# Segment loop of a recurrent-memory attention kernel: one PSUM tile of six banks, projection units interleaved by row chunk, output columns split 256 + 384

## The chip, the cores and the metric

The kernel runs on one core of a Trainium2 chip. The metric is the device time of one execution in microseconds (us), as a median of runs. The profile is one execution recorded by the hardware profiler; its times are us unless marked ns. Engines are TensorE (PE, with its weight loads as PEld), VectorE (DVE), ScalarE (ACT), GpSimd (POOL) and SyncE (SP).

## The reference, cut to what matters

Two attentions over 2048 rows of width 640 are mixed by a gate. Part B is a sliding, dilated attention. Part A, which the change touches, is a recurrence: 64 segments of 32 rows, each preceded by 8 memory rows that the segment before computed, 32 heads of width 192.

```python
for s in range(n_seg):
    h = jnp.concatenate([mem, x[:, 32*s:32*s + 32]], axis=1)      # 8 + 32 rows
    q, k, v = (jnp.einsum('btd,dhe->bhte', h, W) for W in (Wq, Wk, Wv))
    scores = jnp.einsum('bhqe,bhke->bhqk', q, k) * scale          # masked
    o = jnp.einsum('bhqk,bhke->bhqe', softmax(scores), v)
    o = jnp.einsum('bhte,hed->btd', o, Wo)
    mem = o[:, :8];  outs.append(o[:, 8:])
out = g * concatenate(outs) + (1 - g) * B
```

So segment s + 1 can't start before the memory rows of segment s are there: the 64 segments run one after the other.

## The kernel before, in words

Part B and a prepass (projections of the last 8 rows of each segment, called z, which need no memory) come first; then `part_a` runs the 64 segments in a loop that Python unrolls, and `part_z` finishes the output rows of z. In the loop the order of PE, ACT and DVE is the order in which the code is written; DMAs and POOL are placed by the framework, which also writes the semaphore waits, from which tile each instruction reads and writes.

**Projections.** Q, K and V of a segment are nine units (`q`, `k`, `v`, each with u = 0, 1, 2). A unit is 5 row chunks (kc) of 4 matmuls (L771), which work side by side on four strips of 32 columns and put 128 x 512 sums in one PSUM bank. The weights lie in SBUF, except for 14 pieces of 384 KB (`STREAM`) that are read again in each segment through a ring of five buffers (`get_unit`, L569, on SP's queue).

**Order of one segment.** Units Q0 and K0 begin (L957, L958); `sel_b` (L951) turns the last memory rows into lhsT; Q0, K0, Q1, K1 are finished one after the other, and each is copied out of PSUM by ACT (`c_qk`, L784). Q2 begins, then PE transposes the first four copies (`t_qk`, L792) and DVE places them (`c_t`, L803, L807). K2 follows, then scores of half 0 (`s_a`, `s_b`, L825, L834), exp on ACT (`e_exp`, L843), the DMA of V of z (`load_vz`, L756), the last two transposes, V0, sums (`e_norm`, L857), reciprocal as Ln and Exp on ACT (L862, L863) and two DVE multiplies (L869, L870), the same for half 1, V1, V2, and for each half `pv_half` (L897, L902) with its copies `c_x` (L911) and `c_z` (L918). V's copies (`c_v`, L881) are DVE's. The output product (`o_group`, L940) takes 48 chunks for columns 0 to 383 ("oa") and again for 384 to 639 ("ob"). ACT copies each sum to `whi` (L1030, L1038); from it `sel` makes the next segment's memory rows: chunks 0 to 2 from oa, chunks 3 and 4 from ob. `tail` and `store` finish the output rows.

**PSUM.** Three pools with two buffers each: `psm` (one bank: Q, K, V sums, output sums), `psx` (one bank: transposes, half of `pv_half`, `ps_a`), `psS` (two banks: K0, scores, other half of `pv_half`, `ps_mem`). Each use takes a tile of its own.

Of the kernel before, what the change touches and what calls it, by code (L numbers as in the profile page):

```python
# [14 lines left out]
STREAM = (("k", 0, 2), ("q", 1, 1), ("k", 1, 2), ("q", 2, 1), ("q", 2, 4), ("k", 2, 4), ("v", 0, 0), ("v", 1, 0), ("v", 1, 3),  # L15
          ("v", 2, 2), ("oa", 0), ("ob", 0), ("oa", 5), ("ob", 7))
# [13 lines left out]
class _K:  # L30
# [466 lines left out]
    def weights_setup(self):  # L497
        nc, tc, KC = self.nc, self.tc, self.KC
        rest = []
        for m in "qkv":  # L500
            ks = sorted(range(KC), key=lambda kc: (len(self.units(m, 0, kc)) < 3, kc)) if m == "k" else range(KC)
            rest += [(m, J, kc) for kc in ks for J in range(4)]
        rest += [k for k in [("oa", i) for i in range(12)] + [("ob", i) for i in range(8)] if k not in STREAM]
        n = (0, N_EARLY, -N_MID - N_V - N_LAST, -N_V - N_LAST, -N_LAST, None)
        self.early, *self.late = [rest[n[x]:n[x + 1]] for x in range(5)]
        self.W = {m: W.rearrange("(c p) f -> p c f", p=128) for m, W in zip("qkv", (self.Wq, self.Wk, self.Wv))}
        self.wres = self.ctx.enter_context(tc.tile_pool(name="wres", bufs=1))
        self.res_tiles = {}
        self.ahead = {}
        self.after = mybir.DependencyInfo(mybir.DependencyClass.Sync, mybir.DependencyReason.DATA)  # L510
        self.wstream = self.ctx.enter_context(tc.tile_pool(name="wstream", bufs=WBUFS))
        self.wscr = dict(zip(STREAM, self.dram.tile([len(STREAM), 128, 1536], BF, name="wscr")))

    def tile_of(self, pool, k):
        n = 1536 if k[0] in ("oa", "ob") else 512 * len(self.units(*k))
        t = pool.tile([128, n], BF, name="w_" + "_".join(map(str, k)))
        self.res_tiles[k] = t if n < 1536 or k[0] in ("q", "k", "v") else t[:].rearrange(
            "p (c f) -> p c f", c=4 if k[0] == "oa" else 6)
        return t
# [13 lines left out]
    def wo_slice(self, k, dst):  # L533

        n, f0, f1 = (4, 0, 384) if k[0] == "oa" else (6, 384, 640)
        src = self.Wo.rearrange("(c p) f -> p c f", p=128)[:, :, f0:f1]
        return dst.rearrange("p (c f) -> p c f", c=n), src[:, n * k[1]:n * k[1] + n]

    def wo_place(self, part, c):

        n = 4 if part == "oa" else 6
        return c // n, c % n
# [177 lines left out]
    def part_a(self):  # L720
# [4 lines left out]
        with ctx:  # L725
# [3 lines left out]
            VU = [self.TZ[:, 512 * u:512 * u + 512] for u in range(3)]  # L729
            stage = VU + [self.TZ[:, 1920:2432]]  # L730
            KTz = self.TZ[:, 1536:1920].rearrange("p (c k) -> p c k", k=32)
            E0, Vz, zst = self.TZ[:, 1920:2144], self.TZ[:, 2176:2560], self.TZ[:, 1984:2368]
# [5 lines left out]
            k_runs = ([(0, 4, stage[3])], [(0, 1, self.TZ[:, 2432:2560]), (1, 4, ZB[:, 0:384])], [(0, 4, VU[2])])  # L738
            q_runs = ([(0, 4, 2, 0)], [(0, 2, 2, 16), (2, 4, 1, 0)], [(0, 4, 1, 8)])
            KTs = [[z[:, f0 + 128 * x:f0 + 128 * x + 128] for x in range(n)] for z, f0, n in (  # L740
                (self.TZ, 1920, 5), (ZB, 0, 3), (self.TZ, 1024, 4))]
# [4 lines left out]
            psm = ctx.enter_context(tc.tile_pool(name="psm", bufs=2, space=bass.MemoryType.PSUM, reuse_waits="tile"))  # L746
            psx = ctx.enter_context(tc.tile_pool(name="psx", bufs=2, space=bass.MemoryType.PSUM, reuse_waits="tile"))
            psS = ctx.enter_context(tc.tile_pool(name="psS", bufs=2, space=bass.MemoryType.PSUM, reuse_waits="tile"))
# [14 lines left out]
            for s in range(nseg):  # L763
                pqs, sts, pTs, pSs = {}, {}, {}, {}

                def project(ps, m, u, kcs):
                    for kc in kcs:
                        st = self.get_unit((m, u, kc)) if (m, u, kc) in STREAM else None
                        for j in range(4):
                            rhs = self.res(m, j, kc, 512 * u, 512) if st is None or j == 3 else st[:, 512 * j:512 * j + 512]  # L770
                            nc.tensor.matmul(ps[32 * j:32 * j + 32, :], lhsT=hT[:, kc, :], rhs=rhs, start=(kc == 0),  # L771
                                             stop=(kc == KC - 1), tile_position=(0, 32 * j), skip_group_check=True)

                def m_qk(i, kcs):
                    if i not in pqs:
                        pqs[i] = psS.tile([128, 2, 512], F32, tag="S", name="ps_qk")[:, 0, :] if i == 1 else \
                            psm.tile([128, 512], F32, tag="m", name="ps_qk")
                    project(pqs[i], ("q", "k")[i % 2], i // 2, kcs)

                def c_qk(i):  # L780

                    assert i - 4 not in sts
                    sts[i] = stage[i % 4]
                    nc.scalar.copy(sts[i], pqs[i][:])  # L784
# [34 lines left out]
                def s_a(R, chunks):  # L819
                    h, r = R // 2, R % 2  # L820
                    if h not in pSs:
                        pSs[h] = psS.tile([128, 2, 512], F32, tag="S", name="ps_S")
# [49 lines left out]
                pvs = {}  # L872

                def m_v(u, kcs=range(KC)):
                    if u not in pvs:
                        pvs[u] = psm.tile([128, 512], F32, tag="m", name="ps_v")
                    project(pvs[u], "v", u, kcs)

                def c_v(u):
                    for f0, f1 in ((0, 256), (256, 512)) if u == 1 else ((0, 512),):  # L880
                        nc.vector.tensor_copy(VU[u][:, f0:f1], pvs[u][:, f0:f1])  # L881

                def pv_half(h):
                    E = Es[h]
                    pS = psS.tile([128, 2, 512], F32, tag="S", name="ps_oT")
                    px = [psx.tile([128, 512], F32, tag="x", name="ps_oT") for _ in range(2)]
                    pos = [pS[:, 0], px[0], pS[:, 1], px[1]]
                    po = [pos[j][:, 0:240].rearrange("p (r t q) -> p r t q", r=2, t=3) for j in range(4)]
                    full, half = ((0, 0, 0, 128), (2, 1, 256, 384)), ((1, 0, 128, 192), (1, 1, 192, 256))
                    for r, chunks in ((0, full), (1, full), (2, full), (0, half), (1, half), (2, half)):  # L890
                        for t, par, f0, f1 in chunks:
                            p0 = 64 if f0 == 192 else 0
                            for j in range(4):
                                ks = slice(32 * j, 32 * j + 32)
                                out = po[j][p0:p0 + f1 - f0]
                                if r < 2:
                                    nc.tensor.matmul(out[:, r, t, :], lhsT=V[2 * h + r][ks, f0:f1],  # L897
# [25 lines left out]
                pso = {}  # L923

                def o_group(part, i2):
                    n = 384 if part == "oa" else 256
                    if i2 == 0:
                        pso[part] = psm.tile([128, 512], F32, tag="m", name="ps_wo")
                    for jj in range(4):
# [3 lines left out]
                        if (part, i) not in osl:  # L933
# [5 lines left out]
                            osl[part, i] = w[:].rearrange("p (c f) -> p c f", c=4 if part == "oa" else 6)  # L939
# [6 lines left out]
                def sel(part, hT_next, pm):  # L946

                    m0, m1 = (0, 3) if part == "oa" else (3, KC)
                    p = 0 if part == "oa" else 1
                    for m in range(m0, m1):  # L950
                        nc.tensor.matmul(pm[:, p, 8 * (m - m0):8 * (m - m0) + 8], lhsT=whi[:, m * 128:(m + 1) * 128],  # L951
                                         rhs=self.sel_m[:], start=(m == m0), stop=(m == m1 - 1),
                                         skip_group_check=True)
                    nc.vector.tensor_copy(hT_next[:, m0:m1, 0:8], pm[:, p, 0:8 * (m1 - m0)].rearrange(  # L954
                        "p (m i) -> p m i", i=8))

                m_qk(0, (0, 1, 2))  # L957
                m_qk(1, (0, 1))  # L958
                if sel_b is not None:
                    sel_b()  # L960
                m_qk(1, (2,))
                if tail is not None:
                    tail()
                m_qk(0, (3, 4)); c_qk(0)
                m_qk(1, (3, 4)); c_qk(1)
                if store is not None:
                    store()
                m_qk(2, range(KC)); c_qk(2)
                m_qk(3, range(KC)); c_qk(3)
                m_qk(4, (0, 1))  # L970
# [5 lines left out]
                m_qk(4, (2, 3, 4)); c_qk(4)  # L976
# [3 lines left out]
                m_qk(5, range(KC)); c_qk(5)  # L980
# [3 lines left out]
                load_vz(s)  # L984
# [4 lines left out]
                m_v(0)  # L989
                c_v(0)  # L990
# [10 lines left out]
                m_v(1, (0,))  # L1001
# [4 lines left out]
                m_v(1, (1, 2, 3, 4)); c_v(1)  # L1006
                e_mask(1)
                m_v(2, (0, 1, 2))
                pos = pv_half(0)
                c_x(0, pos, (0, 1, 3), "add")  # L1010
                e_norm(1)
                e_recip_a(1)
                m_v(2, (3, 4)); c_v(2)
                e_recip_b(1)
                c_x(0, pos, (2,), "a")
                c_z(0, pos, (1, 3), "aa")
                c_z(0, pos, (0, 2), "dd")
                for i2 in range(6):
                    o_group("oa", i2)
                pos = pv_half(1)  # L1020
                c_x(1, pos, range(4), "adda")
# [4 lines left out]
                for i2 in range(5):  # L1026
                    o_group("ob", i2)
                for i2 in range(6, 12):
                    o_group("oa", i2)
                nc.scalar.copy(whi[:, 0:384], pso["oa"][:, 0:384])  # L1030
                if s + 1 < nseg:
                    load_z(s + 1)
                    pm = psS.tile([128, 2, 512], F32, tag="S", name="ps_mem")
                for i2 in range(5, 12):
                    o_group("ob", i2)
                    if i2 == 8 and s + 1 < nseg:
                        sel("oa", hT_next, pm)
                nc.scalar.copy(whi[:, 384:640], pso["ob"][:, 0:256])  # L1038
# [28 lines left out]
            self.part_z(psm, osl, last)  # L1067
# [19 lines left out]
    def part_z(self, psm, wo, tail):  # L1087
# [6 lines left out]
        for n in range(4):  # L1094
# [3 lines left out]
            for part, f0, nf in (("oa", 0, 384), ("ob", 384, 256)):  # L1098
                ps = psm.tile([128, 512], F32, tag="m", name="ps_z")
                for c in range(48):  # L1100
                    J, g, t = c // 12, c // 3 % 4, c % 3
                    i, x = self.wo_place(part, c)
                    for q in range(4):
# [3 lines left out]
                                         tile_position=(0, 32 * q), skip_group_check=True)  # L1107
                nc.vector.scalar_tensor_tensor(out=b4[:, f0:f0 + nf], in0=ps[:, 0:nf], scalar=self.gZ[:, n:n + 1],
# [64 lines left out]
```

## Time and profile before

| what | value |
|---|---|
| median of three runs | 1715.4 us (1714.1 to 1718.74) |
| profiled execution, its own time | 1710.89 us |
| its span, first to last instruction | 1709.1 us |
| segments in the loop | 64 |
| distance of the ob copies (ACT L1038) of neighbouring segments | 20.13 us mean, 19.05 us least, 27.02 us the last |
| first and last of these copies | 384.1 us and 1652.3 us |
| DMA in the middle 1000 us | 304 GB/s, most of it the ring of weight pieces |

The page gives time and instructions of each engine, then 40 equal slices of the span; the loop is slices 9 to 38. A row of a group gives line, engine, operation, out<-in and shapes, how often, busy us and mean ns of one, then the idle time ahead of it. A matmul's row lasts longer than its share of PE, since four run side by side; the distance of their starts tells what they cost.

### The profile page before, as it was taken

The numbers are of one execution on the slowest core, as the hardware profiler recorded it, in microseconds if no ns is written. First come the engines' busy times: TensorE is split into PE (matmuls) and PEld (weight loads), VectorE is DVE, ScalarE is ACT, GpSimd is POOL, SyncE is SP. The second block draws the span as 40 slices with busy tenths as digits, with TensorE's granted clock in tenths as the row PEclk, the third lists the DMA queues.
The fourth block names the chain that finished last, engine by engine and source line by source line (L and its number), as shares of the span: only waits on it lengthen the run. The fifth ranks groups of instructions, "written<-read, shape, count | busy, mean of one in ns | idle before, by whom it ended". The sixth has DMA issues, their size and how long they took to land.

```text
span 1709.1 us, 75634 instructions
## 1 busy us (share of the span) xinstructions
PE 1602.0 (94%) x33193; PEld 888.6 (52%) x33209; DVE 697.0 (41%) x2159; ACT 803.7 (47%) x2082; POOL 60.0 (4%) x124
## 2 busy tenths in 40 slices
PE   7887999989999999999999999999999999999989
PEld 4544544445555555555555555555555545555559
DVE  3765333234444443444444443444443334444430
ACT  3877423234455444444454444445444444544450
POOL 2030000000000000000000000000000000000000
PEclk9998899999999999999999999999999999999999
DMA  7798798989999998999999999999999989999981
GB/s 200 188 221 203 217 326 222 262 248 311 310 309 313 306 299 294 307 305 303 308 312 294 300 312 301 298 303 309 306 312 303 296 290 304 310 301 306 301 278 31
DMA packets 307607, 479.43 MB, mean 281 GB/s; under 512 B 100556, under 2 KB 186444, under 8 KB 307276
## 3 DMA queue, kind: packets, MB, share of 16 engines
q1 hardware_dynamic: 208144, 418.12, 75.3%
q10 hardware_dynamic: 99132, 56.46, 11.8%
q8 instruction: 260, 4.26, 1.0%
q14 instruction: 71, 0.58, 0.1%
HBM read 432.76 MB, written 47.23 MB: 281 GB/s over the span
## 4 chain that ended last, share of the span: by engine, by line
PE 81%; DMA 11%; ACT 3%; issue 3%; DVE 1%; SPq 1%; ACTq 0%; DVEq 0%
PE ps_qk L771 25%; PE ps_wo L940 13%; PE ps_v L771 10%; PE ps_pre L622 6%; DMA TZ<-zpk_dram 5%; PE ps_qkT L792 5%; PE ps_S L825 4%; PE ps_oT L897 3%; PE ps_z L1104 3%; PE ps_pre L652 3%; DMA wst<-wscr 2%; ACT ZB L1030 2%; PE ps_bqk L236 1%; PE ps_S L857 1%; PE ps_mem L951 1%
## 5 line engine op out<-in xcount | busy, mean ns | idle before, releaser
L771 PEld LDWEIGHTS <-hT 128*32 128x32 bf16 x11520 | 275.3, 96 | 284.5 <-issue 15.3
L784 ACT CAST TZ<-ps_qk 128x512 bf16<-128x512 f32 x384 | 218.4, 586 | 318.6 <-PE ps_qk L771 318.6
L771 PE MATMUL ps_qk<-w_q,hT 128*32 128x512 bf16 x3264 | 267.7, 383 | 2.8 <-issue 2.8
L771 PE MATMUL ps_qk<-w_k,hT 128*32 128x512 bf16 x3264 | 265.5, 380 | 0.7 <-DVE ZV L81 0.4
L771 PE MATMUL ps_v<-w_v,hT 128*32 128x512 bf16 x3072 | 243.7, 383 | 0.0
L803 DVE COPY ZB<-ps_qkT 128x512 bf16<-128x512 bf16 (+1 forms) x256 | 91.0, 356 | 350.2 <-PE ps_qkT L792 254.0
L940 PEld LDWEIGHTS <-TZ 128*32 128x32 bf16 x6144 | 145.7, 96 | 105.8 <-ACT TZ L911 41.6
L940 PE MATMUL ps_wo<-w_oa,TZ 128*32 128x384 bf16 x2560 | 148.2, 330 | 10.4 <-issue 9.8
L881 DVE CAST TZ<-ps_v 128x512 bf16<-128x512 f32 (+1 forms) x256 | 137.0, 556 | 43.8 <-PE ps_v L771 43.7
L771 PE MATMUL ps_qk<-wst,hT 128*32 128x512 bf16 x1152 | 149.1, 381 | 0.5 <-DMA wst<-wscr 0.4
L911 ACT CAST TZ<-ps_oT 128x192 bf16<-128x192 f32 x256 | 75.8, 322 | 146.8 <-PE ps_oT L902 84.8
L911 DVE CAST TZ<-ps_oT 128x192 bf16<-128x192 f32 x256 | 85.7, 355 | 73.0 <-PE ps_oT L902 71.0
L940 PE MATMUL ps_wo<-w_ob,TZ 128*32 128x256 bf16 x2304 | 107.2, 274 | 8.8 <-issue 8.7
L954 DVE CAST hT<-ps_mem 128x24 bf16<-128x24 f32 x126 | 22.5, 179 | 220.7 <-PE ps_mem L951 220.7
L771 PE MATMUL ps_v<-wst,hT 128*32 128x512 bf16 x768 | 100.1, 385 | 8.9 <-DMA wst<-wscr 8.9
L792 PE MATMUL ps_qkT<-ident,TZ 128*128 128x128 bf16 x1536 | 107.5, 219 | 0.1
L792 PEld LDWEIGHTS <-TZ 128*128 128x128 bf16 x1536 | 88.6, 98 | 27.2 <-issue 27.0
L940 PE MATMUL ps_wo<-wst,TZ 128*32 128x256 bf16 (+1 forms) x1280 | 96.3, 301 | 3.3 <-issue 2.7
L843 ACT ACTIVATE ZB<-ps_S 32x224 bf16<-32x224 f32 x256 | 89.0, 348 | 9.4 <-PE ps_S L834 0.7
L843 ACT ACTIVATE TZ<-ps_S 32x224 bf16<-32x224 f32 x256 | 89.0, 348 | 9.4
L752 POOL COPY TZ<-ZB 128x384 bf16<-128x384 bf16 x64 | 32.6, 510 | 1477.1 <-DMA ZB<-zpk_dram 684.4
L825 PE MATMUL ps_S<-ZB,TZ 64*128 64x160 bf16 (+1 forms) x768 | 82.6, 234 | 0.0
(135 smaller groups left out, 2014.6 us busy)
## 6 DMA issues: line engine op xcount, KB each, us to landing
wst<-wscr SPq DMA_DIRECT2D x896, 384.0 KB
zpk_dram<-ZS ACTq DMA_DIRECT2D x4, 3072.0 KB
ZB<-zpk_dram ACTq DMA_DIRECT2D x64, 192.0 KB
zpk_dram<-ZV ACTq DMA_DIRECT2D x32, 192.0 KB
TZ<-zpk_dram ACTq DMA_DIRECT2D x64, 96.0 KB
oz_dram<-TZ ACTq DMA_DIRECT2D x64, 96.0 KB
w_q<-in_A_Wq_dram SPq DMA_DIRECT2D x14, 384.0 KB
w_k<-in_A_Wk_dram SPq DMA_DIRECT2D x14, 384.0 KB
```

What stands on the lines that cost most here:

```text
L622: nc.tensor.matmul(ps[:], lhsT=weights(j, kc, 6 * Rp + 3 * r + t), rhs=zTi[:, kc, :], start=(kc == 0), stop=(kc == KC - 1))
L652: mm = nc.tensor.matmul(pss[g][:], lhsT=zTi[:, kc, 128 * st:128 * st + 128], rhs=weights(kc, g), start=(kc == 0), stop=(kc == KC - 1))
L771: nc.tensor.matmul(ps[32 * j:32 * j + 32, :], lhsT=hT[:, kc, :], rhs=rhs, start=(kc == 0), stop=(kc == KC - 1), tile_position=(0, 32 * j), ...
L784: nc.scalar.copy(sts[i], pqs[i][:])
L792: nc.tensor.transpose(pT[:, 128 * t:128 * t + 128], st[:, 128 * t:128 * t + 128], self.ident[:])
L803: nc.vector.tensor_copy(QTf[:, run[2]:run[2] + 4, run[3]:run[3] + n, :].rearrange("p b x i -> p x b i"), src.rearrange("p (x b i) -> p x b ...
L825: nc.tensor.matmul(grid(h, par)[:, :, 0:80].rearrange("p j (b r i) -> p j b r i", r=2, i=8)[:, :, :, r, :], lhsT=KTs[3 * R + t][k0:k1, :], ...
L843: nc.scalar.activation(E[ps], pSs[h][ps, :, 112 * j:112 * j + 112], ACT.Exp, scale=scale_a)
L881: nc.vector.tensor_copy(VU[u][:, f0:f1], pvs[u][:, f0:f1])
L897: nc.tensor.matmul(out[:, r, t, :], lhsT=V[2 * h + r][ks, f0:f1], rhs=E[ks, par, 0:80].rearrange("p (b r i) -> p b r i", r=2, i=8)[:, :, r ...
L911: cp(oTxs[2 * h + j // 2][:, 6 * (j % 2):6 * (j % 2) + 6, :], pos[j][:, 0:240].rearrange("p (c q) -> p c q", q=40)[:, :, 8:40])
L940: nc.tensor.matmul(pso[part][32 * jj:32 * jj + 32, 0:n], lhsT=oTxs[2 * (g // 2) + J // 2][:, 6 * (J % 2) + 3 * (g % 2) + t, :], rhs=osl[pa ...
```

## The change

- PSUM of the loop becomes one tile `PS` of six banks, taken once: pairs M, A, B. Each unit has its bank: Q0, V0, V2 in the first bank of M and Q1, V1, oa in the second; K0, K1 and scores of half 0 in A; Q2, K2, scores of half 1 and ob in B. `pv_half(0)` uses A, `pv_half(1)` B and one bank of M. `psx` stays a pool; `ps_mem` moves to it.
- All six Q, K units take row chunk 0, then all take chunk 1; `sel_b` stands between, `tail` behind. Then Q0, K0 are finished together, then Q1, K1, then Q2, K2. V is interleaved likewise.
- Copies are spread: c_qk(1) and c_qk(3) go to DVE, c_v(2) and half of c_v(1) to ACT; each copy to `whi` is halved between ACT and DVE.
- oa has columns 0 to 255, ob 256 to 639; `sel` gives chunks 0, 1 from oa and 2 to 4 from ob. oa and ob take turns.
- V of z lies in bytes 1024 to 1407 of `TZ`, and `load_vz` stands behind the first four transposes. Other bytes of `TZ` and `ZB` are dealt out anew.
- `STREAM` names 14 other pieces of the same size. In `part_z` oa and ob take turns by chunk and are copied after both.

```diff
-            psm = ctx.enter_context(tc.tile_pool(name="psm", bufs=2, space=bass.MemoryType.PSUM, reuse_waits="tile"))
+            psp = ctx.enter_context(tc.tile_pool(name="psp", bufs=1, space=bass.MemoryType.PSUM, reuse_waits="tile"))
             psx = ctx.enter_context(tc.tile_pool(name="psx", bufs=2, space=bass.MemoryType.PSUM, reuse_waits="tile"))
-            psS = ctx.enter_context(tc.tile_pool(name="psS", bufs=2, space=bass.MemoryType.PSUM, reuse_waits="tile"))
+            PS = psp.tile([128, 6, 512], F32, name="PS")
+            M, A, B = PS[:, 0:2], PS[:, 2:4], PS[:, 4:6]
+            acc = {("q", 0): M[:, 0], ("k", 0): A[:, 0], ("q", 1): M[:, 1], ("k", 1): A[:, 1], ("q", 2): B[:, 0],
+                   ("k", 2): B[:, 1], ("v", 0): M[:, 0], ("v", 1): M[:, 1], ("v", 2): M[:, 0]}
+            pso = {"oa": M[:, 1], "ob": B[:, 1]}
+            pSs = (A, B)
...
-                    nc.scalar.copy(sts[i], pqs[i][:])
+                    (nc.vector.tensor_copy if i in (1, 3) else nc.scalar.copy)(sts[i], acc["qk"[i % 2], i // 2])
...
-                        nc.vector.tensor_copy(VU[u][:, f0:f1], pvs[u][:, f0:f1])
+                        (nc.scalar.copy if f0 or u == 2 else nc.vector.tensor_copy)(VU[u][:, f0:f1], acc["v", u][:, f0:f1])
...
+                rounds((0,), Q0, K0, Q1, K1, Q2, K2)
                 if sel_b is not None:
                     sel_b()
+                rounds((1,), Q0, K0, Q1, K1, Q2, K2)
                 if tail is not None:
                     tail()
+                rounds((2, 3, 4), Q0, K0); c_qk(0); c_qk(1)
                 if store is not None:
                     store()
+                rounds((4, 3, 2), Q1, K1); c_qk(2); c_qk(3)
+                rounds((2, 3), Q2)
                 for i in range(4):
                     t_qk(i)
                 c_t(0); c_t(1)
                 c_t(2, (0,)); c_t(3, (0,))
                 c_t(3, (1,))
+                load_vz(s)
+                rounds((4,), Q2, K2); c_qk(4)
...
+                rounds((3, 2), K2); c_qk(5)
+                rounds((2,), V0)
                 s_a(0, HALF); s_a(1, HALF); s_b(0, HALF)
                 s_a(0, FULL); s_a(1, FULL); s_b(0, FULL)
                 e_exp(0)
-                load_vz(s)
                 t_qk(4); t_qk(5)
...
+                rounds((0, 1), V0, V1)
+                rounds((3, 4), V0); c_v(0)
...
+                rounds((2, 3, 4), V1); c_v(1)
                 e_mask(1)
+                rounds((4, 0, 1), V2)
                 pos = pv_half(0)
+                c_x(0, pos, (0, 1), "ad")
+                rounds((2,), V2)
                 e_norm(1)
                 e_recip_a(1)
+                rounds((3,), V2); c_v(2)
+                c_z(0, pos, (1,), "d")
+                c_x(0, pos, (3,), "d")
+                c_z(0, pos, (3,), "d")
                 e_recip_b(1)
                 c_x(0, pos, (2,), "a")
+                c_z(0, pos, (0, 2), "ad")
+                for i2 in range(4):
                     o_group("oa", i2)
+                    o_group("ob", i2)
                 pos = pv_half(1)
+                c_x(1, pos, (0, 1, 3, 2), "adad")
                 c_z(1, pos, range(4), "adad")
...
+                for i2 in (4, 5):
+                    o_group("oa", i2)
                     o_group("ob", i2)
                 for i2 in range(6, 12):
                     o_group("oa", i2)
+                nc.scalar.copy(whi[:, 0:128], pso["oa"][:, 0:128])
+                nc.vector.tensor_copy(whi[:, 128:256], pso["oa"][:, 128:256])
...
+                for i2 in range(6, 12):
                     o_group("ob", i2)
+                    if i2 == 9 and s + 1 < nseg:
                         sel("oa", hT_next, pm)
+                nc.scalar.copy(whi[:, 256:448], pso["ob"][:, 0:192])
+                nc.vector.tensor_copy(whi[:, 448:640], pso["ob"][:, 192:384])
```

## The prediction

> **What bounds the kernel now.** I read the page first, for the shares, then the stretches of the loop, then one segment in the timeline.
>
> ```profile
> PE 1602.0 (94%) x33193; PEld 888.6 (52%) x33209; DVE 697.0 (41%) x2159; ACT 803.7 (47%) x2082; POOL 60.0 (4%) x124
> ...
> PEclk9998899999999999999999999999999999999999
> ...
> PE 81%; DMA 11%; ACT 3%; issue 3%; DVE 1%; SPq 1%; ACTq 0%; DVEq 0%
> ```
>
> PE is busy all through the loop, at full clock, and carries 81% of the chain that ended last; ACT and DVE work under half of the time. They do it beside PE, as the timeline of the shortest segment (19.05 us) shows:
>
> ```profile
> 1496.08 0.28 PE L834 MATMUL ps_S<-ZB,TZ 128*128 128x128 bf16 x2
> ...
> 1496.29 0.62 PE L771 MATMUL ps_v<-w_v,hT 128*32 128x512 bf16 x8
> ...
> 1496.39 1.43 ACT L843 ACTIVATE ZB<-ps_S 32x224 bf16<-32x224 f32 x4
> ...
> 1496.74 1.03 PE L771 MATMUL ps_v<-w_v,hT 128*32 128x512 bf16 x13
> ...
> 1497.39 0.76 DVE L881 CAST TZ<-ps_v 128x256 bf16<-128x256 f32 x2 [0.62 <-PE ps_v L771]
> ```
>
> While ACT takes 1.43 us for the exp of half 1, PE goes on with V (rows at 1496.29 and 1496.74). Nothing holds it: scores and V's sum lie in PSUM tiles of their own. The ring of weights isn't the bound either: its queue waits for buffers that PE has not yet freed.
>
> ```profile
> SPq L569 <- PE ps_wo L940: 238.3, 196, 3.2
> SPq L569 <- PE ps_qk L771: 219.3, 239, 2.2
> ```
>
> **What the change removes.** Three waits of PE. In 44 segments with all rows recorded the mean is 20.03 us. PE waits for V of z (L902) 0.23 us a segment on average; for oa's copy to `whi`, after the 16 matmuls meant to cover it, about 0.22; and ahead of `pv_half(1)` about 0.18. The first goes, since the transfer, whose packets end 3.1 to 5.5 us after its issue, is asked for some 6 us ahead of its use instead of 4.5; the second goes, since the copy is halved and ob's groups behind it are 0.163 us, not 0.109. That is 0.6 us a segment, 38 us in 64.
>
> **What it adds.** I read the order of the built program with its waits, and counted each semaphore's increments up to the value awaited, to see who releases whom. All six banks are now one tile, and every access to it is ordered behind the latest access to it by another engine, whatever the bank. PE's first matmul of Q1, chunk 4 (second bank of M), waits for DVE's copy of K0 (first of A), which itself waits for ACT's copy of Q0. V0, chunk 0, waits for the exp of half 0; V1, chunk 2, for that of half 1; the next segment's first matmul waits for DVE's half of the ob copy, which waits for ACT's half. None of these stood in the program before. So each read of PSUM by ACT or DVE stops PE, and since PE works in order, all that follows stands behind it, and with it the next segment.
>
> Prices are from rows: copies of 128x512 are 0.585 us on ACT (L784) and 0.69 on DVE (L881), of 256 columns 0.37 and 0.42, of 192 columns 0.325 and 0.36 (L911), of 48 columns 0.21 and 0.20 (L918); four exps 1.43 (L843); Ln and Exp together 0.61 (L862, L863); the two multiplies 0.45 (L869, L870). In the timeline an engine's copy starts 0.21 us after the last group of a unit has streamed, another engine goes on 0.04 after it, PE 0.06 after it. The waits of a segment, in order:
>
> - whi of ob, two halves in turn: 0.21 + 0.325 + 0.04 + 0.36 + 0.06 = 1.00
> - c_qk(0) then c_qk(1): 0.21 + 0.585 + 0.04 + 0.69 + 0.06 = 1.59; c_qk(2), c_qk(3) the same
> - c_qk(4): 0.21 + 0.585 + 0.06 = 0.86; c_qk(5) the same
> - exp of half 0: 0.20 + 1.43 + 0.06, less 0.54 of transposes that may run = 1.15
> - c_v(0) ahead of the sums: 0.21 + 0.69 + 0.06 = 0.96
> - sums to scores of half 1: 0.29 + 0.61 + 0.04 + 0.45 + 0.06 = 1.45
> - exp of half 1: 0.11 + 1.43 + 0.06 = 1.60
> - c_v(1), two halves in turn: 0.21 + 0.42 + 0.04 + 0.37 + 0.06 = 1.10
> - c_x of strip 0: 0.23 + 0.325 + 0.06 = 0.62
> - Ln and Exp of half 1: 0.28 + 0.61 + 0.06 = 0.95
> - c_v(2), multiplies, c_x, c_z on ACT, c_z on DVE, each behind the one before: 0.21 + 0.585 + 0.04 + 0.45 + 0.04 + 0.325 + 0.11 + 0.24 + 0.06 = 2.06
> - c_x and c_z of half 1: 0.23 + 0.72 + 0.04 + 0.31 + 0.06 = 1.36
> - whi of oa: 0.21 + 0.27 + 0.04 + 0.29 + 0.06 = 0.87; 128 columns on each engine aren't in the trace, so they lie between the rows of 48 and 192 columns, and I take the middle
>
> The sum is 18.0 us. PE's own work is the shortest segment, 19.05, less the waits that still stood in it (0.5) and some 0.4 of array drain that the 0.21 above counts already: 18.15. So a segment takes **36.2 us at full clock**. The other edits move nothing here: the same matmuls, the same 14 pieces of 384 KB, and at half the pace the ring has time to spare.
>
> **The clock.** PE would work half the time, in bursts, so I looked at how the clock answered idle stretches. Columns are PE, PEld, DVE, ACT, POOL busy (instructions), clock, DMA share, GB/s:
>
> ```profile
> 899.33:902.74 3.41, 1.63 (x43) 1.06 (x46) 0.18 (x1) 0.48 (x1) 0.00 (x0) 1.00 0.92 272
> 902.75:906.16 3.41, 3.41 (x38) 1.21 (x34) 0.56 (x2) 0.37 (x1) 0.51 (x1) 0.50 0.61 188
> ...
> 1640.03:1643.43 3.40, 2.30 (x24) 0.73 (x27) 0.94 (x3) 0.00 (x0) 0.00 (x0) 0.50 0.98 355
> 1643.44:1646.85 3.41, 3.41 (x91) 1.73 (x88) 1.91 (x7) 1.32 (x6) 0.00 (x0) 0.50 1.03 351
> ...
> 476.07:479.48 3.41, 1.86 (x82) 1.04 (x81) 1.43 (x5) 1.04 (x6) 0.00 (x0) 1.00 0.87 323
> ```
>
> A stretch of 3.41 us with 1.63 us of PE was followed by one at half clock; one with 1.86 was not. At half clock, 2.30 us of PE didn't bring the full clock back; 3.41 did. In my sum PE works 3.3 us of the 12.1 between c_v(0) and the first output group, 0.9 in a stretch of 3.41, so the clock falls there in every segment. It comes back only after a nearly full stretch, the first of which is in the two rounds that open the next segment. Half clock then doubles what lies between: most of V1 and V2, `pv_half`, the scores of half 1 and all of the output product, 6.9 us of work, and 3.4 to 6.8 us of time in the next segment's rounds, some 2.5 us of work. 36.2 + 6.9 + 2.5 = **45.6 us a segment**. The bounds are 36.2 (clock full) and 36.2 + 18.15 = 54.3 (never back).
>
> The page "TensorE: Matmul & The Clock Gate" of the Trainium skill, part 1, says that the clock halves after an idle window of some 3.4 us and sums it up as no PE idle gap above 3.4 us. My longest wait is 2.06 us, so by that rule the clock would stay full. The stretch at 899.33 with 1.63 us of PE in it disagrees.
>
> **Sum.** 45.6 - 20.03 = 25.6 us a segment, in 64 segments 1638. `part_z` reads the same tile: its next block waits for both DVE operations of the one before (0.48 + 0.62 us, L1108), three times, and the last end has one more, some 4 us. The profiled execution took 1710.9, which is 0.3% under the median of 1715.4; 1710.9 + 1638 + 4 = 3353. I forecast **3350 us**.
>
> **The rivals.**
>
> - *Waits as above, clock full.* Each wait is under 2.1 us, so if short gaps don't count as idle: 64 x (36.2 - 20.03) + 4 = 1039, 2750 us. For it: stretches with 1.86 to 2.3 us kept the clock. Against: the row of 1.63.
> - *Clock never back.* 54.3 a segment: 3910 us. It needs the opening rounds (8.5 us at half clock) to hold no nearly full stretch of 3.41; they do hold one.
> - *Not slower: the waits are already over when PE comes to them.* Then only the three removed waits count, and the place is the end of a segment and `pv_half`: 1710.9 - 38 = 1673 us. It decides where the copy awaited has ended before PE reaches the matmul, so where other PE work of at least 0.9 us stands between. In the changed order no such work stands there: the awaiting matmul follows the read's own source directly (transposes, 0.54 us, are the one exception). The page "PSUM — Partial Sum Buffer" of the Trainium skill, Specifications, says that ScalarE and VectorE can access PSUM in parallel while no bank collides. That speaks for it, as far as the banks go; semaphores written into the program hold all the same.
>
> **Chances.** Forecast with the clock partly half 0.78 (own range 3050 to 3620: stalls 10% off are 115 us, the clock's return one stretch off is 110); clock full 0.12; never back 0.05; not slower 0.04; something unnamed 0.01. The range takes in the full clock: 2720 to 3620. A measurement of this kernel tells 0.3% from no change; faster 0.03, same 0.01, slower 0.96.
>
> **What would show it.** In the changed profile PE's gaps ahead of Q1 chunk 4, V0 chunk 0 and V1 chunk 2 should name DVE's copy of K0 and ACT's exps, about 1.6, 1.2 and 1.6 us; ahead of a segment's first matmul 1.0 us of `whi`. PE's share falls to about half at full clock, the slices of the clock to 0.6 to 0.8, DMA to some 130 GB/s, and ring waits nearly vanish. The wait for V of z (L902) is gone. I am wrong if PE's first matmul of Q1 chunk 4 follows K0's last at once, or if the slices show a full clock.

## The result, and the profile after

The changed kernel takes **3246.1 us** (median of 4 runs, 3243.8 to 3246.8) against 1714.8 (4 runs) of the kernel before: ratio 1.893, 95% interval 1.888 to 1.899. The forecast was 3350, its range for the likeliest case 3050 to 3620. The page of the profiled execution, engines, clock slices and chain:

```profile
span 3242.0 us, 76034 instructions
...
PE 2185.5 (67%) x33209; PEld 1100.3 (34%) x33209; DVE 790.0 (24%) x2415; ACT 783.1 (24%) x2018; POOL 59.8 (2%) x124
...
PEclk9999867777666777666777666776666776667778
...
PE 65%; ACT 17%; DVE 10%; issue 3%; DMA 2%; ACTq 2%; SPq 0%; DVEq 0%
```

PE executes the same matmuls as before (33209 recorded, 33193 before, where some records are missing), yet the loop runs at 0.6 to 0.8 of the clock, and ACT and DVE, 4% of the chain before, now hold 27% of it. The waits of PE between 700 and 2900 us (engine and line, who released it: us in total, times, longest) name them:

```profile
PE PS L780 <- DVE TZ L789: 141.4, 100, 1.4
PE PS L932 <- DVE TZ L914: 94.0, 49, 1.9
PE PS L780 <- ACT ZB L846: 78.2, 50, 1.6
PE PS L780 <- ACT TZ L789: 68.6, 100, 0.7
```

L780 is the projections' matmul, L932 the output product's, L789 `c_qk`, L846 exp, L914 `c_z`. One such place, in the timeline:

```profile
2830.30 0.38 PE L780 MATMUL PS<-w_k,hT 128*32 128x512 bf16 x4
2830.74 0.58 ACT L789 CAST TZ<-PS 128x512 bf16<-128x512 f32 x1 [6.46 <-PE PS L780]
...
2831.36 0.69 DVE L789 CAST TZ<-PS 128x512 bf16<-128x512 f32 x1 [1.53 <-ACT TZ L789]
2832.11 0.40 PE L780 MATMUL PS<-w_q,hT 128*32 128x512 bf16 x4 [1.42 <-DVE TZ L789]
```

K0's last group, ACT's copy of Q0, DVE's copy of K0 and Q1's chunk 4 stand one behind the other, although they use three banks and three engines. DVE doesn't even copy beside ACT: both read the one tile. As before, the ring waits for PE and not PE for the ring, only longer: with `SPq L569 <- PE PS L780: 1312.5, 498, 6.2` and the output product's row its queue waits 1925 of these 2200 us, where it waited 754 of 1000 before. So the sign that ring waits nearly vanish did not come. No wait for V of z is left.

From the 10th of the 64 segments on, nearly every one takes 44.37 us, to 0.01 us. Stretches of 3.41 us over one segment, laid on the edges where the clock changes (columns as in the prediction):

```profile
1510.62:1514.03 3.41, 2.72 (x24) 0.98 (x24) 0.87 (x2) 0.00 (x0) 0.00 (x0) 0.50 0.53 145
1514.03:1517.44 3.41, 1.15 (x20) 0.87 (x20) 0.51 (x3) 1.38 (x5) 0.00 (x0) 1.00 0.13 51
1517.44:1520.86 3.42, 1.77 (x16) 0.60 (x19) 0.61 (x2) 0.96 (x3) 0.00 (x0) 0.50 0.29 77
...
1537.92:1541.34 3.42, 3.42 (x35) 1.17 (x32) 0.18 (x1) 0.00 (x0) 0.00 (x0) 0.50 0.20 43
1541.34:1544.75 3.41, 2.46 (x48) 1.08 (x41) 0.65 (x2) 0.58 (x1) 0.00 (x0) 1.00 0.62 213
1544.75:1548.16 3.41, 1.53 (x28) 0.74 (x31) 1.11 (x2) 0.58 (x1) 0.00 (x0) 1.00 0.75 213
...
1551.58:1554.99 3.41, 1.66 (x28) 1.23 (x29) 1.15 (x5) 1.98 (x5) 0.00 (x0) 1.00 0.76 195
1554.99:1558.40 3.41, 2.73 (x24) 1.00 (x24) 0.87 (x2) 0.00 (x0) 0.00 (x0) 0.50 0.45 132
```

The pattern repeats after 13 stretches: 13 x 3.413 = 44.37. Eight of them are at half clock. The full clock is lost twice a segment: in the stretch with the exp of half 0 (1551.58) and, after one stretch at half clock, in that with the reciprocals and the exp of half 1 (1514.03).

### The profile page after: what moved, and what is told of

The parts are those of the page before. It is cut to its first block, busy times and chain, and to the rows that moved or that the text cites. A ratio compares the mean times of both kernels' runs of the same rounds, so it can differ in the third digit from the quotient of the medians.

```text
span 3242.0 us, 76034 instructions
## 1 busy us (share of the span) xinstructions
PE 2185.5 (67%) x33209; PEld 1100.3 (34%) x33209; DVE 790.0 (24%) x2415; ACT 783.1 (24%) x2018; POOL 59.8 (2%) x124
## 4 chain that ended last, share of the span: by engine, by line
PE 65%; ACT 17%; DVE 10%; issue 3%; DMA 2%; ACTq 2%; SPq 0%; DVEq 0%
PE PS L780 32%; PE PS L932 14%; ACT TZ L789 5%; PE ps_pre L622 3%; ACT ZB L846 3%; DVE TZ L789 3%; PE PS L828 3%; DVE TZ L877 2%; PE ps_qkT L797 2%; ACT TZ L877 2%; ACT TZ L907 2%; PE PS L893 2%; PE PS L1100 2%; PE ps_pre L652 2%; ACT TZ L846 2%
## 5 line engine op out<-in xcount | busy, mean ns | idle before, releaser
L780 PEld LDWEIGHTS <-hT 128*32 128x32 bf16 x11520 | 372.9, 111 | 1107.5 <-issue 962.9
L780 PE MATMUL PS<-w_v,hT 128*32 128x512 bf16 x3072 | 459.5, 606 | 212.5 <-ACT TZ L846 68.3
L780 PE MATMUL PS<-w_q,hT 128*32 128x512 bf16 x3072 | 424.8, 456 | 233.5 <-DVE TZ L789 181.1
L780 PE MATMUL PS<-w_k,hT 128*32 128x512 bf16 x3456 | 419.6, 431 | 44.0 <-ACT TZ L789 44.0
L780 PE MATMUL PS<-wst,hT 128*32 128x512 bf16 x1920 | 314.4, 475 | 143.8 <-ACT ZB L846 100.0
L932 PEld LDWEIGHTS <-TZ 128*32 128x32 bf16 x6144 | 241.6, 135 | 382.7 <-issue 234.2
L932 PE MATMUL PS<-w_oa,TZ 128*32 128x256 bf16 x2688 | 235.1, 415 | 200.5 <-DVE TZ L914 122.8
L789 ACT CAST TZ<-PS 128x512 bf16<-128x512 f32 x256 | 149.8, 585 | 796.7 <-PE PS L780 792.1
L932 PE MATMUL PS<-w_ob,TZ 128*32 128x384 bf16 x2304 | 279.9, 517 | 44.6 <-DVE ZB L1025 44.6
L932 PE MATMUL PS<-wst,TZ 128*32 128x384 bf16 (+1 forms) x1152 | 161.1, 487 | 0.0
L789 DVE CAST TZ<-PS 128x512 bf16<-128x512 f32 x128 | 88.5, 691 | 241.9 <-ACT TZ L789 241.9
L846 ACT ACTIVATE ZB<-PS 32x224 bf16<-32x224 f32 x256 | 89.0, 348 | 97.6 <-PE PS L837 95.4
L846 ACT ACTIVATE TZ<-PS 32x224 bf16<-32x224 f32 x256 | 89.0, 348 | 84.4 <-PE PS L837 82.1
```

The lines of the kernel that those rows point to most:

```text
L780: nc.tensor.matmul(acc[m, u][32 * j:32 * j + 32, :], lhsT=hT[:, kc, :], rhs=rhs, start=(n == 1), stop=(n == KC), tile_position=(0, 32 * j) ...
L789: (nc.vector.tensor_copy if i in (1, 3) else nc.scalar.copy)(sts[i], acc["qk"[i % 2], i // 2])
L846: nc.scalar.activation(E[ps], pSs[h][ps, :, 112 * j:112 * j + 112], ACT.Exp, scale=scale_a)
L932: nc.tensor.matmul(pso[part][32 * jj:32 * jj + 32, 0:n], lhsT=oTxs[2 * (g // 2) + J // 2][:, 6 * (J % 2) + 3 * (g % 2) + t, :], rhs=osl[pa ...
```

## The experiments

The theory (**one tile**): PE waits for copies of other banks because the six banks are one tile, and these waits cost the clock. Rivals: **order** (the interleaved chunks, the other streamed pieces or the split cost the time), and **clock no cause** (waits alone).

**Own tiles.** All edits kept but one, and banks are tiles; over A and B two pools are opened in turn, one with two single-bank tiles, one with the two-bank score tile. The edit not kept: the first four groups of oa come ahead of the first four of ob, where the change lets them take turns.

```diff
-            PS = psp.tile([128, 6, 512], F32, name="PS")
+            M = [psp.tile([128, 512], F32, name=f"ps_M{x}") for x in range(2)]
...
+                t = [p.tile([128, 512], F32, name=f"ps_{'AB'[h]}{x}") for x in range(2)]
...
+                pSs[h] = pool_of(h, 2).tile([128, 2, 512], F32, name=f"ps_S{h}")
```

> All edits of the change kept, but the six banks are tiles of their own: M0 and M1 one bank each, the K/Q accumulators of each pair as single-bank tiles, and the two-bank score tiles from pools opened over the same banks. The first four groups of the oa columns come ahead of the first four of ob, so that ob's bank is free by then. One-tile theory (the waits between PE and the copies of other banks, and the half clock they bring, are the whole loss): the segment loses the 0.6 us that the other edits save, 20.03 to about 19.4 us, time 1677 us, between 1660 and 1715. Order theory (the interleaved row chunks, the streamed slices or the 256 + 384 split cost the time): 3000 us or more.

Measured 1702.5 us, ratio to before 0.995 (0.993 to 0.997). The order theory falls: with the same copies, pieces and split, and the same order but for those four groups, the 1530 us are gone (a run below has the order of the change to the letter and takes 1690.1 us). The time lies inside the range, but 25 us above the 1677 expected. The waits of PE from 600 to 1600 us show one left:

```profile
PE ps_B L953 <- DVE ZB L894: 22.8, 50, 0.6
PE ps_M L953 <- issue: 10.6, 11, 2.0
PE ps_B L953 <- issue: 2.9, 4, 0.9
```

ob's first group waits for the multiplies (L894), as the score tile over its bank is given up only then.

**One tile in the kernel before.** Only the pools go; `psm`'s tiles become the first two banks in turn, `psS`'s the other two pairs in turn:

```diff
-            psm = ctx.enter_context(tc.tile_pool(name="psm", bufs=2, ...))
-            psS = ctx.enter_context(tc.tile_pool(name="psS", bufs=2, ...))
+            PS = psp.tile([128, 6, 512], F32, name="PS")
...
+                return PS[:, used["m"] % 2]
...
+                x = 2 + 2 * (used["S"] % 2)
+                return PS[:, x:x + 2]
```

> The kernel before with its order, its loads and its copies untouched; only its four pool slots (two of one bank, two of two) become slices of one six-bank tile, taken in the same rotation. One-tile theory: six Q/K copies at some 0.86 us, exp 1.15 and 1.60, V copies 0.96 and 1.10, the reciprocal chains 1.45 and 0.95, attention copies 0.62, 2.06 and 1.36, whi and state copies about 2.1, together 18.8 us of waits beside 19.05 of PE work, and a half clock over part of it as in the kernel after (9.4 us): 41 to 48 us a segment, time 3050 to 3500 us. Order theory: 1715 us, as before, since no order changes.

Measured 3191.8 us, 43.31 us a segment. One edit, with nothing else changed, makes 1.865 (1.855 to 1.875) of the time. Its first wait rows, again 600 to 1600 us:

```profile
PE PS L781 <- ACT TZ L794: 80.6, 115, 0.8
PE PS L950 <- DVE TZ L928: 45.6, 23, 2.0
PE PS L781 <- DVE TZ L891: 39.8, 46, 1.3
```

ACT's copies (L794), which PE passed freely before, hold it 115 times in 23 segments, 0.8 us at most.

**Idle matmuls in the waits**, and the same kernel without them:

```diff
+                def fill(n):
...
+                        for _ in range(n * FILL):
+                            nc.tensor.matmul(fills[0][:], lhsT=self.ident[:], rhs=self.res("v", 3, 0, 0, 512),
+                                             start=True, stop=True, skip_group_check=True)
```

> The kernel after with 60 idle matmuls a segment (128x512, identity by a resident weight, into a bank of their own that nobody reads) set into its waits, in counts that fit each wait at full clock (6, 6, 3, 3, 4, 3, 6, 6, 4, 2, 4, 9, 6, 4 less rounding): 60 x 0.213 us = 12.8 us of PE time within 18 us of waits. To free the bank, the two attention outputs of a half that lay in the small pool move into the six-bank tile. No work is left out. If the clock's halving is part of the loss as the prediction has it (36.2 us a segment at full clock against 44.4 now): the clock stays full and the time falls to 2720 to 2850 us. If the clock is no cause, only the waits: no lower than the same kernel without the idle matmuls, and higher by up to 12.8 x 64 = 820 us where they do not fit.

> The same kernel as the one with idle matmuls, with none of them: the bank set aside, the two attention outputs moved into the six-bank tile. Both theories: about the kernel after, 3100 to 3350 us; it is the base for the run with the idle matmuls.

Measured 2888.6 us with them and 3262.1 without. With 13 us more PE work in each segment (60 x 0.216), segments take 38.47 us instead of 44.39. The pages' clock slices, first with, then without:

```profile
PEclk9989989999999999999999999999999999999999
```

```profile
PEclk9999867777767776767776767777767777677778
```

So the half clock is part of the loss, and the clock answers to PE's work. The time came out 40 us above the range given, probably because some fills outlast their waits; which ones was not looked at.

**Three tiles of two banks.**

```diff
-            PS = psp.tile([128, 6, 512], F32, name="PS")
-            M, A, B = PS[:, 0:2], PS[:, 2:4], PS[:, 4:6]
+            M, A, B = [psp.tile([128, 2, 512], F32, name=f"PS_{x}") for x in "MAB"]
```

> The kernel after with its six banks as three two-bank tiles (M, A, B), all else the same: a middle dose. Waits that the program still has between banks of one tile: Q1's chunk 4 behind both copies of the first pair (0.7 us), K2 behind the copy of Q2 (0.9), V2 behind the second half of V1's copy (1.1), oa behind V2's copy on ScalarE (1.2), oa's group 4 behind the attention copies of half 1 (1.4): 5.3 us a segment, less 0.65 that the run with own tiles had and this one covers. Theory that time goes by the waits: clock full, 1702 + 4.6 x 64 = 2000 us, between 1880 and 2100. Theory that a shared tile costs something else, by access: near 3246.

Measured 1962.3 us, 24.09 us in nearly every segment, the clock full in the loop. The five waits read from the program are the five in the trace (600 to 1600 us, some 41 segments):

```profile
PE PS_M L779 <- ACT TZ L876: 49.3, 41, 1.2
PE PS_M L931 <- ACT TZ L876: 43.9, 41, 1.4
PE PS_M L931 <- ACT TZ L913: 43.1, 41, 1.1
PE PS_B L779 <- ACT TZ L788: 28.9, 42, 0.7
PE PS_M L779 <- ACT TZ L788: 19.8, 42, 0.5
```

Time goes by the waits: 5.24 us a segment here against 18.9 in the kernel after. With no more than that, the clock holds.

**Undivided copies to `whi`**, in the kernel after (ob's is shown, oa's likewise):

```diff
-                nc.scalar.copy(whi[:, 256:448], pso["ob"][:, 0:192])
-                nc.vector.tensor_copy(whi[:, 448:640], pso["ob"][:, 192:384])
+                nc.scalar.copy(whi[:, 256:640], pso["ob"][:, 0:384])
```

> The kernel after, with the two copies into whi undivided on ScalarE (384 columns 0.5 us where the two halves one behind the other took 0.7; 256 columns 0.4 for 0.6): 0.4 us less of waits a segment. If waits add up: 3246 - 0.4 x 64 = 3220 us. If the segment is tied to a whole number of clock windows (13 x 3.413 = 44.37 us in the kernel after): 3246 unchanged, or a step of about 3.4 x 64 = 218 us.

Measured 3060.1 us. Neither number: the two waits shrink by 0.66 us a segment together, and the segment from 44.37 to 41.25 on average, now between 40.4 and 43.9. Half clock falls from 61% to 50% of the time between 600 and 1800 us. So the 44.37 us were one settled pattern among others, and a small edit moved 2.5 us of half clock besides its 0.66. Why the pattern of the kernel after settles at 13 stretches stays open.

**The score tile given up early**, on own tiles, so that ob waits for nothing. Sums, reciprocals and the second half's output then use a single-bank tile, and oa and ob take turns again from the first group:

```diff
                 e_exp(1)
+                banks[1] = singles(1)
                 rounds((2, 3, 4), V1); c_v(1)
...
                 c_z(0, pos, (0, 2), "ad")
-                banks[1] = singles(1)
```

> As the kernel with own tiles, in the order of the change to the letter (oa and ob groups by turns), and with the two-bank score tile of half 1 given up right after exp: sums, reciprocals and the second half's attention output use a single-bank tile of the same bank, so that ob's first groups no longer wait for the multiplies of half 1. In the run with own tiles PE lost 0.65 us a segment there. Theory that this wait is all that ate the edits' gain: 1702 - 0.65 x 64 = 1660 us, between 1640 and 1685. Theory that the other edits are worth nothing and the saving was bought elsewhere: 1695 to 1710 us, no change against the run with own tiles.

Measured 1690.1 us, ratio to before 0.989 (0.986 to 0.992): the fastest complete kernel so far, but 30 us over the forecast. The shortest segment fell as expected, from 19.35 to 18.68 us; the mean only from 19.99 to 19.80. What came late next are rows in which PE waits for nothing but its own instruction stream (600 to 1600 us):

```profile
PE ps_M L953 <- issue: 14.3, 12, 1.9
PE ps_B L953 <- issue: 12.6, 13, 2.4
PE ps_mem L964 <- issue: 2.6, 2, 1.7
```

Most lie at every 256th PE instruction, and PE goes on 1.1 to 1.6 us after a packet of the instruction queue (q8) has ended. Gaps above 0.45 us at these places, between 400 and 1600 us: 33 with 36.6 us in the kernel before, 24 with 23.7 with own tiles, 52 with 62.0 here.

**Without the streamed pieces**, here and in the kernel before:

```diff
+                            gone = (m, u, kc) in STREAM and 1 <= s < nseg - 2
-                            rhs = self.res(m, j, kc, 512 * u, 512) if st is None or j == 3 else ...
+                            rhs = self.res(m, 3 if gone else j, kc, 512 * u, 512) if st is None or j == 3 else ...
```

> The kernel with own tiles and the score tile given up early, without the streamed weights in segments 1 to 61: fourteen 384 KB loads a segment are left out, and the matmuls that used them take a resident slice of the same shape. So the output is another one; instructions on PE, ACT and DVE are as before. In the run with the loads, 52 stalls at every 256th PE instruction took 62 us between 400 and 1600 us, and the shortest segment was 18.68 us beside a mean of 19.80. Theory that the streamed loads delay the instruction packets (they share the DMA engines): the stalls vanish, nearly every segment takes 18.7 to 18.9 us, time 1690 - 61 x 1.05 = 1626 us, between 1610 and 1640. Theory that PE fetches too slowly by itself at this pace: segments stay near 19.8 us, time 1675 to 1690 us.

> The kernel before with the same loads left out in segments 1 to 61 (its output too is another one). By the first theory: segments at the shortest of before, 19.05 us, or lower where z's V and the stalls took time even there; time 1714 - 61 x 1.0 = 1653 us, between 1640 and 1665, and the difference to the own-tile kernel without loads is what the edits save on PE alone: 61 x 0.37 = 23 us. By the second theory: 1700 to 1715 us.

Measured 1630.9 and 1650.3 us. The stalls shrink to 6 with 4.8 us (400 to 1550 us) in the first; in the second no gap of over 0.6 us is left. Most segments take 18.69 and 19.05 us. The middle 1000 us, with the pieces and without:

```profile
500.00:1500.00 1000.00, 960.54 (x22600) 548.70 (x22593) 498.85 (x1676) 468.57 (x1371) 25.87 (x51) 1.00 0.93 309
```

```profile
500.00:1500.00 1000.00, 997.09 (x23663) 570.98 (x23665) 523.09 (x1758) 491.93 (x1441) 26.88 (x53) 1.00 0.12 31
```

At a DMA share of 0.93 PE is busy for 96% of the time; at 0.12 for 99.7%. So the streamed loads bring the stalls, and the packets show how. There is one of 16 KB for every 256 PE instructions. It takes no longer with the loads (median 0.97 us with them, 1.04 without), but it starts later. Counted from the moment PE enters the block of 256 ahead of the one that the packet brings, the median start is at 1.99 us with the loads and at 0.28 without; one packet in ten starts after 3.6 us with them, after 1.4 without. The page "DMA: Bandwidth & Descriptors" of the Trainium skill, section on queues, rings and completion order, says that a DMA engine takes turns between its queues, one packet at a time; that fits, but the traces kept don't say on which DMA engine a packet stood, so turn-taking as the cause of the late start isn't shown.

**Two edits undone, on the fastest kernel**: the load of V of z behind exp again, and the copies to `whi` undivided.

```diff
-                load_vz(s)
                 rounds((4,), Q2, K2); c_qk(4)
...
                 e_exp(0)
+                load_vz(s)
```

> As the kernel with own tiles and the score tile given up early, with one edit of the change undone: the load of z's V asked for behind exp, as in the kernel before, no longer behind the transposes. Its bytes stay the new ones. Forecast of that edit's worth: 0.23 us a segment, 15 us: slower by 5 to 20 us than the same kernel with the early load. Theory that the load is hidden either way: the same within 4 us.

> As the kernel with own tiles and the score tile given up early, with one edit undone: the copies into whi undivided on ScalarE. Forecast of that edit's worth: about 0.22 us a segment at oa's copy, nothing at ob's: 14 us, so 1695 to 1710 us beside 1690. Theory that stalls of the instruction stream take up any such gain: within 5 us of 1690.

Measured 1701.6 and 1690.5 us beside 1690.1. The late load brings back PE's wait for V of z (`PE ps_A L919 <- DMA TZ<-zpk_dram: 11.9, 20, 1.2`, 600 to 1600 us) and costs 11.5 us by the medians; the two ratios to before, 0.989 (0.986 to 0.992) and 0.993 (0.990 to 0.996), overlap, so its size is uncertain. The halved copies bring nothing: undivided, the short segments are even 0.15 us shorter (18.53, met several times, and 18.44 once, beside 18.68), and the time is the same.

## Why the prediction was right, and where its sizes were off

Matched start by start against the same PE instructions of the own-tile kernel without pieces (18.64 us a segment at full clock), a segment of 44.37 us splits in three:

| term, us a segment | forecast | measured |
|---|---|---|
| PE's own work | 18.15 | 18.64 |
| waits | 18.0 | 18.9 |
| work at half clock | 9.4 | 6.8 |
| sum | 45.6 | 44.4 |

- **The mechanism, one tile orders all accesses**: right, shown in both directions by own tiles (1702.5) and by one tile in the kernel before (3191.8).
- **The list of waits**: all fifteen are in the trace and no other above 0.3 us. Eleven came within 0.14 us of the forecast, most within 0.06: the c_qk pairs 1.59 and 1.58 for 1.59, the exps 1.14 for 1.15 and 1.63 for 1.60, and the furthest off, sums to scores of half 1, 1.31 for 1.45. The other four make up the 0.9 us missing, and in each PE was at half clock as it ended its last group: c_v(1) 1.43 for 1.10, the chain from c_v(2) 2.30 for 2.06, `whi` of ob 1.19 for 1.00, of oa 1.01 for 0.87. The turnarounds had been read from a timeline at full clock.
- **PE's own work**: 18.64 where 18.15 was forecast. The forecast took 0.9 us off the shortest segment of 19.05, 0.5 for waits still in it and 0.4 for array drain. No row gives the 0.4, and without pieces the changed order needs only 0.4 less than 19.05 in all.
- **The clock**: that it falls in each segment and comes back in the opening rounds was right; the term was mis-sized. "Half clock then doubles what lies between" failed in the following: the opening rounds lost 1.6 us, not 2.5; `pv_half` hardly slows (0.2 us over both halves, its matmuls stream only 40 columns); the scores of half 1 lay in the one stretch at full clock. V lost 2.2 us, the output product 2.8. And the clock falls earlier than said, first in the stretch with the exp of half 0.
- **The rule of the Trainium skill** (page "TensorE: Matmul & The Clock Gate", part 1: no PE idle gap above 3.4 us) would have left the clock full, 2750 us. No wait in a settled segment exceeds 2.3 us, and half clock held for 61% of the time. The measurement decides against it as a rule for one gap; the free-running window of 3413 ns, which the same part states, agrees with the edges seen.
- **Removed waits, 0.6 us a segment**: hidden here, so seen on own tiles. Without pieces, 19.05 against 18.69: 0.36 us, on PE alone, with no wait for V of z on either side; which edits save it was not taken apart. V of z came to 11.5 us by the medians, where 0.23 x 64 = 15 was forecast. The halved copy, named as a reason, brings none of it.
- **The ring**: the prediction cleared it, since its queue waits for PE. That reading holds, but without the pieces the kernel before takes 1650.3 us against 1711.6 in the same series. So the ring cost some 61 us all the same: about 37 in stalls of PE's instruction stream, which the prediction did not name, and part of the rest in the waits for V of z, which are gone too.
- **Which term carried the miss**: the loop's mean is 44.20 us, as the first segments are shorter (40.8 to 44.3); 64 x (45.6 - 44.2) = 90 of the 104 us by which the forecast was too high. The terms' errors partly cancel (+0.5, +0.9, -2.6): that the sum came within some 3% is in part luck. `part_z` and the end grew by 6 us where 4 was forecast.

## What to carry to other kernels

A framework that orders accesses by tile makes banks of one tile into one lock. Before banks are merged into one tile, read the waits of the built program; each read by ACT or DVE in the middle of PE's stream cost its own duration plus about 0.3 us here. And when PE waits are removed from a kernel whose DMA engines are over 90% busy, expect stalls of PE's instruction stream to take part of the gain back, as the 62 us above did.

## What the runs showed of the hardware that was not expected

- **What the clock answers to is work in a stretch of 3.413 us, not a gap.** Counted by the streaming time of the columns (0.216 us for 512 at full clock, twice that at half), in four kernels with one tile: between 400 and 2800 us, at full clock every stretch with more than 1.34 us of streaming kept it, every one with less than 1.22 lost it; at half clock every one with more than 2.52 brought it back, none with less than 2.32 did. In the kernels without one tile, where few stretches lose it, two with 1.36 and 1.38 us did. The profile's busy time doesn't order them: above, 1.53 us kept the clock and 1.66 lost it, for it counts the whole row of each short matmul (0.18 us for the 40 columns of `pv_half`, which stream in 0.02).
- **Useless work can pay**: 60 idle matmuls a segment took 374 us off (3262.1 to 2888.6).
- **A loop can settle on a whole number of these stretches**: 13 of them for some 55 segments, until an edit worth 0.66 us moved it by 3.1.
